# Attention into two gated layers: softmax sums applied where layer 1 loads x, and six w_out chunks homed with the first layer's w_in

## The chip, the cores and the metric

The kernel runs on one core of one Trainium2 chip. The metric is the device time of one execution in microseconds (us). The engines are TensorE (PE), VectorE (DVE), ScalarE (ACT), GpSimd (POOL) and SyncE (SP); SP issues every DMA of this kernel.

## What is computed

The cut reference: windowed causal attention in fp32 (batch 4, 8 heads, 576 tokens, 64 columns a head, window 128), whose output x of 2304 x 512 goes through a layer with a rational gate and then one with a squared ReLU.

```python
scores = np.where(mask, scale * q @ k.T + bias, -1e9)
attn = np.exp(scores - scores.max(-1))
attn = attn / (attn.sum(-1) + 1e-09)
x = (attn @ v)                       # to (2304, 512)
h = x @ w_in                         # 512 x 2048
g = (a0 + a1*h + a2*h**2 + a3*h**3) / (1 + |b0|*|h| + |b1|*h**2 + 1e-6)
x = g @ w_out                        # 2048 x 512
out = (np.maximum(x @ w2_in, 0)**2) @ w2_out
```

## The kernel before

**Attention** runs in 16 pairs p (batch, two heads) of five query blocks, called units u, 80 in all. For a pair, q, k and v are loaded (`qr`, `kr`, `vr`; three DMAs each, L285 and L292), q and k are transposed on PE (`trq`, `trk`, `trr`) and copied to `qkT`. For a unit, PE makes the scores `s` (L340); DVE adds bias and mask from the table `bias8` and takes the minimum (L351); ACT makes the exponentials `e` with their row sum (L360); DVE turns the sum into a reciprocal (`stats` L368, `rcp` L370); POOL multiplies `e` by it (`norm`, L375, two a unit); PE transposes `e` to `pt` (L391); ACT or DVE copies that to `ptsb`; PE multiplies by v into `o` and, for the last 64 tokens of a pair, `or` (L416 to L429). The copied result `xT` of a pair goes to DRAM as `xs` (L443).

**The layers** run in blocks of up to 512 tokens, 16 steps f a block, the first layer's block 1 of 256. A step makes h (`gemm_in`, L614, twelve matmuls of 512 columns, since operands are split into a high and a low part), the gate on ACT, POOL and DVE, the high part `gh` on ACT and the low part `gl` on DVE (L214), and adds to y (`gemm_out`, L698, twelve matmuls). PSUM has four banks for s and h together, so h of step f+4 waits for `gl` of step f, the last reader of its bank. x of a block is read back from DRAM (`load_x`, tile `xr`, L594) once all pairs that make it are written.

**Weights** come raw as 64-bit numbers, 64 chunks of 512 KB (`win1r`, `wout1r`, ..., L185), and are rebuilt as fp32: `w_exp` on any engine (L191, L194), three bit operations on DVE (L199, L201, L203), the high part (L207, L211), the low part (L214). The 16 chunks of w_in of the first layer are converted during attention. Their home is the pool `wip`. w_out's home `wop` is opened by `attn_end`, in the space that the attention pools free, so its conversion writes nothing before attention's last copies.

**Order.** The class Plan simulates all pieces with a cost for each and puts down, for every engine, one static order; each engine then runs its instructions in that order and waits where an operand is missing. SP is planned at 0.45 us a DMA. A table BIAS decides between pieces that could start at the same time.

Of the kernel before, what the change touches and what calls it, by code (L numbers as in the profile page):

```python
# [8 lines left out]
F32 = mybir.dt.float32  # L9
# [80 lines left out]
BIAS = {'W0': 1143.4, 'W1': -1312.0, 'W2': -103.0, 'W3': 231.6, 'attn_end': -330.6, 'bias': -108.4, 'exp': -122.1, 'g1': 74.7, 'g2': 539.3, 'gh': -139.2, 'gl': -251.1, 'ldk': 347.8, 'ldk0': -524.7, 'ldq': -531.4, 'ldq0': -320.3, 'ldv': 478.2, 'norm': -28.5, 'ptc': 550.8, 'ptp': -190.6, 'pv': 8.0, 'r_abs': -768.2, 'r_g1': 208.6, 'r_g2': -228.1, 'r_g3': -464.7, 'r_p1': -223.8, 'r_p2': -200.3, 'r_r1': -323.9, 'r_r2': -709.6, 'r_t1': 437.4, 'r_t2': 344.1, 'r_u': -364.3, 'rcp': -339.7, 's': 671.8, 's_g': -202.9, 's_relu': 313.4, 'scl': 1.6, 'scp': -406.8, 'stats': -279.6, 'trk': -947.3, 'trk0': 180.7, 'trk0c': -287.8, 'trkc': -54.6, 'trq': -411.2, 'trq0': 156.9, 'trq0c': 381.4, 'trqc': 386.6, 'trr': -605.2, 'trrc': -29.2, 'ttr': -13.0, 'w0': -272.4, 'w1': 518.7, 'w2': -17.8, 'w3': -48.3, 'w4': -107.7, 'w5': -1964.8, 'warm': 652.0, 'wl': -312.2, 'x': 515.5, 'xh': 551.8, 'xl': 139.5, 'xld': 247.8, 'xo': -326.7, 'xr': -322.8, 'yc': 281.2, 'yo': 224.4}  # L90
# [4 lines left out]
VB, TRO = 3, 0  # L95
# [3 lines left out]
def tile_window_attention_moe_moe(  # L99
# [43 lines left out]
    ]  # L143

# [98 lines left out]
    bias8 = acst.tile([P, H, 2 * P], F32, name="bias8")  # L243
# [26 lines left out]
    st = {}  # L270


    def parts(p, nme):
        return [(0, 2), (2, NQ - 1)] if p == 0 and nme != "v" else [(0, NQ - 1)]

    def load_tok(p, nme, src, t0, t1):
# [12 lines left out]
        if t1 == NQ - 1:

            rows = slice(P - LAST, P) if nme == "v" else slice(0, LAST)
            nc.sync.dma_start(  # L292
                t[rows, t1, :, :],
                src[b, h0 : h0 + 2, MAIN:, :].rearrange("h p d -> p h d"),
            )


    def tr_main_pe(p, nme, t0, t1):
        ps = bank("tr", f"tr{nme}{p}_{t0}")
        src = st[p][nme]  # L300
        for t in range(t0, t1):
            nc.tensor.transpose(  # L302
                ps[:, t * P : (t + 1) * P], src[:, t].rearrange("p h d -> p (h d)"), ident
            )
        if "qkT" not in st[p]:
            st[p]["qkT"] = ap2.tile([P, 2, S], F32, tag="qkT", name=f"qkT{p}")
        cs = slice(t0 * P, t1 * P)
        st[p]["trps"] = (ps[:, cs], st[p]["qkT"][:, "qk".index(nme), cs])

    def tr_rem_pe(p):  # L310
        ps = bank("tr", f"trr{p}")
        for n, nme in enumerate("qk"):
# [29 lines left out]
    def ttr(u, j):  # L342
# [4 lines left out]
        if j == 0:  # L347
            d["st"] = ae.tile([P, 8], F32, tag="st", name=f"st{u}")
            d["e"] = ae.tile([P, 2, 2 * P], F32, tag="e", name=f"e{u}")
        b0 = P if i == 0 else 0  # L350
        nc.vector.tensor_tensor_reduce(  # L351
            d["e"][:rows, j, :w], d["s"][j], bias8[:rows, h, b0 : b0 + w],
            -0.125, 1e30, ALU.add, ALU.min, d["st"][:rows, j : j + 1],
        )

    def exp(u, j):
        d = us[u]
        rows, w, s = d["rows"], d["w"], d["st"]
        e = d["e"][:rows, j, :w]
        nc.scalar.activation(  # L360
            e, e, AF.Exp, scale=-1.0, bias=s[:rows, j : j + 1],
            accum_out=s[:rows, 2 + j : 3 + j],
        )

    def stats(u, k):
        rows, s = us[u]["rows"], us[u]["st"]
        if k == 0:
            nc.vector.tensor_scalar(s[:rows, 4:6], s[:rows, 2:4], 1e-9, None, ALU.add)  # L368
        else:
            nc.vector.reciprocal(s[:rows, 4:6], s[:rows, 4:6])  # L370
# [33 lines left out]
    def pv_pe(u):  # L404
# [4 lines left out]
        if i == NQ - 1:  # L409
            st[p]["or"] = bank("tr", f"or{p}")  # L410
# [39 lines left out]
    for p in range(NP):  # L450
# [5 lines left out]
        for n, (nme, src) in enumerate((("q", q), ("k", k), ("v", v))):  # L456
            if n == 2:
                busy = [("pv", u0 - VB * NQ + NQ - 1)]
            else:
                busy = [("trr", p - 2)]  # L460
            for t0, t1 in parts(p, nme):
                part = "" if t1 == NQ - 1 else "0"
# [25 lines left out]
        plan.add(  # L488
            ("trr", p), lambda p=p: tr_rem_pe(p), PE=0.2,
            after=[("trkc", p), ("xr", p - 2)], prio=u0 - 3,  # L490
        )
        plan.add(("trrc", p), lambda eng, p=p: tr_copy(p, eng), ACT=0.16, DVE=0.2, after=[("trr", p)], prio=u0 - 3)
# [364 lines left out]
```

## Time and profile before

| | |
|---|---|
| time, median of 3 runs | 952.62 us (952.4 to 954.46) |
| profiled execution, time | 952.25 us |
| profiled execution, span | 950.5 us |
| PE busy | 935.9 us |
| DVE busy | 627.5 us |
| ACT busy | 495.0 us |
| POOL busy | 395.0 us |

Attention fills the first 150 us or so, the two layers the rest. The span is what the hardware profiler saw of the program; the profiled execution's own time is 1.75 us longer. The profile's views used below: the page (busy time, chain of work that ended last, groups of instructions), a table by stretch, the waits of an engine, the timeline of single instructions, and the DMA issues.

### The profile page before, as it was taken

Reading aid. Unit: us, or ns where it says so; the run is one execution under the profiler, and the core shown is the slowest. Engines: PE = TensorE matmul, PEld = TensorE weight load, DVE = VectorE, ACT = ScalarE, POOL = GpSimd, SP = SyncE. Lnnn points to the kernel's source line nnn. Section 1 sums busy time; section 2 is a strip of 40 time slices with the busy share of each in tenths; the row PEclk is TensorE's granted clock in tenths of the full one; section 3 lists DMA queues with packets and bytes.
Section 4 is the critical chain, followed back from the end, with each engine's and each line's share of the span. In section 5 each row is a group of like instructions: output and inputs, shape, how many; then the busy total and the mean of one; then the engine's idle time right before and its main releaser. Section 6 shows DMA issues by size and latency. Waiting matters only on the chain.

```text
span 950.5 us, 14368 instructions
## 1 busy us (share of the span) xinstructions
PE 935.9 (98%) x4940; PEld 760.1 (80%) x4940; DVE 627.5 (66%) x1436; ACT 495.0 (52%) x1089; POOL 395.0 (42%) x481
## 2 busy tenths in 40 slices
PE   8999999899999999999999999999999999999998
PEld 6666667688998888888888888888888888888887
DVE  5999999999987877777999977762222223222332
ACT  5888896667776655655676543432222222222222
POOL 5787887677555436334767753230010001000100
PEclk9999999999999999999999999999999999999999
DMA  6989763222401100200142236412000200010010
GB/s 150 239 203 231 205 169 101 90 83 92 154 22 37 32 1 1 89 1 1 45 136 87 66 117 197 130 45 90 0 1 1 89 1 0 35 33 1 1 45 23
DMA packets 96521, 72.24 MB, mean 76 GB/s; under 512 B 61888, under 2 KB 84416, under 8 KB 96448
## 3 DMA queue, kind: packets, MB, share of 16 engines
q1 hardware_dynamic: 96448, 71.33, 26.3%
q8 instruction: 39, 0.64, 0.3%
q14 instruction: 34, 0.28, 0.1%
HBM read 57.15 MB, written 14.16 MB: 75 GB/s over the span
## 4 chain that ended last, share of the span: by engine, by line
PE 90%; DVE 6%; POOL 1%; ACT 1%; issue 1%; DMA 1%; POOLq 0%; ACTq 0%; DVEq 0%
PE y L698 40%; PE h L614 40%; PE s L340 3%; PE pt L391 3%; PE o L416 2%; DVE e L351 1%; PE warm L549 1%; POOL e L375 1%; DVE h L667 1%; PE trk L302 1%; PE trq L302 1%; ACT e L360 1%; DVE wb L203 1%; DVE wb L201 0%; DMA win1r<-in_moe_w_in_dram 0%
## 5 line engine op out<-in xcount | busy, mean ns | idle before, releaser
L214 DVE TENSOR_TENSOR gl<-h,gh 128x512 fp32r<-128x512 f32 (+1 forms) x160 | 101.1, 633 | 115.3 <-ACT gh L207 115.2
L207 ACT ACTIVATE gh<-h 128x512 fp32r<-128x512 f32 (+1 forms) x160 | 88.5, 554 | 162.4 <-PE y L698 152.7
L675 DVE SCALAR_TENSOR_TENSOR h<-h,ah 128x512 f32<-128x512 f32 (+1 forms) x80 | 51.6, 645 | 112.5 <-ACT ah L671 112.5
L614 PE MATMUL h<-xh,win1hi 128*128 128x512 f32 (+1 forms) x320 | 119.0, 372 | 4.6 <-DVE gl L214 4.6
L211 POOL TENSOR_SCALAR xh<-xr 128x512 fp32r<-128x512 f32 (+1 forms) x20 | 12.5, 629 | 255.5 <-PE h L614 253.9
L614 PE MATMUL h<-xl,win1hi 128*128 128x512 f32 (+1 forms) x320 | 118.4, 370 | 0.1
L614 PE MATMUL h<-xh,win1lo 128*128 128x512 f32 (+1 forms) x320 | 118.2, 369 | 0.0
L614 PE MATMUL h<-xh,win2hi 128*128 128x512 f32 (+1 forms) x320 | 117.9, 368 | 0.0
L614 PE MATMUL h<-xh,win2lo 128*128 128x512 f32 (+1 forms) x320 | 117.7, 368 | 0.0
L698 PE MATMUL y<-gl,wout1hi 128*128 128x512 f32 (+1 forms) x320 | 117.7, 368 | 0.0
L698 PE MATMUL y<-gh,wout1hi 128*128 128x512 f32 (+1 forms) x320 | 117.7, 368 | 0.0
L614 PE MATMUL h<-xl,win2hi 128*128 128x512 f32 (+1 forms) x320 | 117.7, 368 | 0.0
L698 PE MATMUL y<-gh,wout1lo 128*128 128x512 f32 (+1 forms) x320 | 117.7, 368 | 0.0
L698 PE MATMUL y<-wout2hi,gh 128*128 128x512 f32 x288 | 112.1, 389 | 0.0
L698 PE MATMUL y<-wout2hi,gl 128*128 128x512 f32 x288 | 112.1, 389 | 0.0
L639 POOL TENSOR_SCALAR t<-ah,ab_sb 128x512 f32<-128x512 f32 (+1 forms) x80 | 64.2, 803 | 115.2 <-ACT ah L627 98.8
L698 PE MATMUL y<-wout2lo,gh 128*128 128x512 f32 x288 | 112.0, 389 | 0.0
L671 ACT ACTIVATE ah<-h 128x512 f32<-128x512 f32 (+1 forms) x80 | 44.4, 554 | 122.9 <-PE h L614 122.7
L641 POOL TENSOR_TENSOR t<-t,ah 128x512 f32<-128x512 f32 (+1 forms) x80 | 99.8, 1247 | 6.2
L375 POOL TENSOR_SCALAR e<-e,st 128x256 f32<-128x256 f32 (+2 forms) x160 | 85.4, 549 | 29.2 <-ACT e L360 12.0
L627 ACT ACTIVATE ah<-h 128x512 f32<-128x512 f32 (+1 forms) x80 | 44.2, 553 | 64.5 <-PE h L614 64.0
L647 DVE TENSOR_TENSOR u<-u,h 128x512 f32<-128x512 f32 (+1 forms) x80 | 50.3, 629 | 39.1 <-ACT u L631 39.0
(114 smaller groups left out, 1991.8 us busy)
## 6 DMA issues: line engine op xcount, KB each, us to landing
win1r<-in_moe_w_in_dram SPq DMA_DIRECT2D x16, 512.0 KB, 4.3
wout1r<-in_moe_w_out_dram SPq DMA_DIRECT2D x16, 512.0 KB, 3.4
win2r<-in_moe_w_in_dram SPq DMA_DIRECT2D x16, 512.0 KB, 3.7
wout2r<-in_moe_w_out_dram SPq DMA_DIRECT2D x16, 512.0 KB, 3.4
xs<-xT SPq DMA_DIRECT2D x16, 288.0 KB, 3.0
out_dram<-yt SPq DMA_DIRECT2D x18, 256.0 KB, 2.1
vr<-in_v_dram SPq DMA_DIRECT2D x32, 128.0 KB, 4.1
ys<-yt SPq DMA_DIRECT2D x16, 256.0 KB, 4.2
```

What stands on the lines that cost most here:

```text
L207: nc.scalar.activation(dst, src, AF.Copy)
L214: (nc.vector if eng == "DVE" else nc.gpsimd).tensor_tensor(dst, a, b, ALU.subtract)
L340: nc.tensor.matmul(dst[j], qT[js, qs], kT[js, k0:k1], start=True, stop=True)
L375: nc.gpsimd.tensor_scalar(e, e, d["st"][: d["rows"], 4 + j : 5 + j], 1.0, ALU.mult, ALU.mult)
L614: nc.tensor.matmul(h[:, :n], a[:, c * P : (c + 1) * P], bb[:, :n], start=(m == 0), stop=(m == 3 * NCC - 1),)
L627: nc.scalar.activation(gt("ah", 2, ji, f), tl["h", ji, f], AF.Abs)
L639: nc.gpsimd.tensor_scalar(gt("t", 2, ji, f), ah, ab_sb[:, 1:2], ab_sb[:, 0:1], ALU.mult, ALU.add)
L641: nc.gpsimd.tensor_tensor(tl["t", ji, f], tl["t", ji, f], ah, ALU.mult)
L647: nc.vector.tensor_tensor(u, u, h, ALU.mult)
L671: nc.scalar.activation(gt("ah", 2, ji, f), tl["h", ji, f], AF.Relu)
L675: nc.vector.scalar_tensor_tensor(h, h, 0.0, tl["ah", ji, f], ALU.max, ALU.mult)
L698: nc.tensor.matmul(dst, a, bb, start=(f == 0 and m == 0), stop=(f == NF - 1 and m == 2))
```

## The change

1. The reciprocal is no longer applied to `e`. `norm` and the two small DVE operations of each unit go. `exp` puts its row sums in a table `sums[p % 3]` (128 x 10); once a pair two DVE operations make the reciprocals `rc`, PE transposes them (into the free part of `or`), ACT or DVE copies them to `rt`, and a DMA writes them to DRAM (`rs`, 16 DMAs). `load_x` of the first layer also loads them, spread over the 64 rows of a head, as tile `R` (two DMAs for each DMA of `xr`), and `norm_x` multiplies `xr` by `R` on DVE or POOL.
2. `wop0` is a home for the first six chunks of w_out that exists from the start; `wop` keeps the other ten. To make room, `e` lives in the tiles of `gh` and `gl`, and the bias table in those of `ah` and `t`.
3. v's loads are planned on their own, the dependences are adapted, BIAS has other values.

```diff
-BIAS = {'W0': 1143.4, 'W1': -1312.0, 'W2': -103.0, ...
+BIAS = {'W0': 149.1, 'W1': 54.9, 'W2': -317.0, ...
...
+    NE = 6
+    wop0 = ctx.enter_context(tc.tile_pool(name="wop0", bufs=NE))
...
-        pool = pools[nme[:-1]]
+        pool = wop0 if nme[:-1] == "wout" and f < NE else pools[nme[:-1]]
...
-    bias8 = acst.tile([P, H, 2 * P], F32, name="bias8")
+    bias8 = [
+        gp.tile([P, 2, 2 * P], F32, tag="at"[k % 2] + "h" * (k % 2 == 0), name=f"bias{k}", bufs=2)
...
-            d["e"] = ae.tile([P, 2, 2 * P], F32, tag="e", name=f"e{u}")
+            d["e"] = gp.tile([P, 2, 2 * P], F32, tag=("gh", "gl")[u % 2], name=f"e{u}", bufs=3)
...
-            accum_out=s[:rows, 2 + j : 3 + j],
-        )
...
-        nc.gpsimd.tensor_scalar(
-            e, e, d["st"][: d["rows"], 4 + j : 5 + j], 1.0, ALU.mult, ALU.mult
-        )
+            e, e, AF.Exp, scale=-1.0, bias=s[:rows, j : j + 1], accum_out=sums[p % 3][:rows, c : c + 1],
+        )
+
+    def rcp(p):
+        t = st[p]["rc"] = ap2.tile([P, 2 * NQ], F32, tag="rc", name=f"rc{p}")
+        nc.vector.tensor_scalar(t, sums[p % 3], 1e-9, None, ALU.add)
+        nc.vector.reciprocal(t, t)
+
+    def r_tr(p):
+        st[p]["or"] = bank("tr", f"or{p}")
+        nc.tensor.transpose(st[p]["or"][: 2 * NQ, P : 2 * P], st[p]["rc"], ident)
+
+    def r_copy(eng, p):
+        t = st[p]["rt"] = ap2.tile([2 * NQ, P], F32, tag="rt", name=f"rt{p}")
+        copy(eng, t, st[p]["or"][: 2 * NQ, P : 2 * P])
+
+    def r_out(p):
+        nc.sync.dma_start(rs[p], st[p]["rt"])
...
-        pools["wout"] = ctx.enter_context(tc.tile_pool(name="wop", bufs=NF))
+        pools["wout"] = ctx.enter_context(tc.tile_pool(name="wop", bufs=NF - NE))
...
+        if jobs[ji][0] == "a":
+            t = tl["R", ji, c] = xp.tile([P, T], F32, tag="R", name=f"R{ji}_{c}", bufs=2)
+            for d, m, _, _, r, q0 in runs(ji, c):
+                for j in range(2):
+                    nc.sync.dma_start(
+                        t[j * D : (j + 1) * D, d : d + m],
+                        bass.AP(tensor=r.tensor, offset=r.offset + j * NQ * P + q0, ap=[[0, D], [1, m]]),
+                    )
+
+    def norm_x(eng, ji, c):
+        n = jobs[ji][2]
+        xr = tl["xr", ji, c][:, :n]
+        (nc.vector if eng == "DVE" else nc.gpsimd).tensor_tensor(xr, xr, tl["R", ji, c][:, :n], ALU.mult)
...
-            0: [], 1: [("attn_end",)], 2: [("g1", NB1 - 1, f)], 3: [("g2", NB1 - 1, f)],
+            0: [], 1: [] if f < NE else [("attn_end",)], 2: [("g1", NB1 - 1, f)], 3: [("g2", NB1 - 1, f)],
```

**POOL, from attention's end into the first gate.** The names: `e` with a number is a unit's exponentials, `t0_0` the denominator of block 0's step 0, `wb` a weight chunk in conversion. Before:

```order
L375 TENSOR_SCALAR e74_2463<-e74_2463,st74_2462 64x192 x2
L375 TENSOR_SCALAR e75_2495<-e75_2495,st75_2494 128x128 x2
L375 TENSOR_SCALAR e76_2507<-e76_2507,st76_2506 128x256 x2
L375 TENSOR_SCALAR e77_2550<-e77_2550,st77_2549 128x256 x2
L375 TENSOR_SCALAR e78_2554<-e78_2554,st78_2553 128x256 x2
L375 TENSOR_SCALAR e79_2578<-e79_2578,st79_2577 64x192 x2
L639 TENSOR_SCALAR t0_0_2651<-ah0_0_2634,ab_sb_96 128x512
L641 TENSOR_TENSOR t0_0_2651<-t0_0_2651,ah0_0_2634 128x512
```

Six units' multiplications stood ahead of `t0_0`. With the change POOL reads there:

```order
L199 TENSOR_SCALAR wb17_2392<-wout1r_1_2312 128x512
L216 TENSOR_SCALAR wout1hi_1_2441<-wb17_2392 128x512
L219 TENSOR_TENSOR wout1lo_1_2442<-wb17_2392,wout1hi_1_2441 128x512
L199 TENSOR_SCALAR wb18_2475<-wout1r_2_2382 128x512
L219 TENSOR_TENSOR wout1lo_2_2531<-wb18_2475,wout1hi_2_2530 128x512
L199 TENSOR_SCALAR wb19_2536<-wout1r_3_2450 128x512
L680 TENSOR_SCALAR t0_0_2550<-ah0_0_2544,ab_sb_115 128x512
L682 TENSOR_TENSOR t0_0_2550<-t0_0_2550,ah0_0_2544 128x512
```

The multiplications of `e` are gone; weight pieces, w_out's among them, stand in their place, and one of them is the row just ahead of `t0_0`.

**DVE, from `gl` of block 0's step 1 to `gl` of step 2.** `u`, `t` and `h` with block and step are the gate's tiles; `wb` and `wout1r` belong to a chunk of w_out. Before, the last twelve of the fourteen rows that end with `gl0_2`:

```order
L203 SCALAR_TENSOR_TENSOR wb18_2823<-wout1r_2_2723,wb18_2823 128x512
L667 SCALAR_TENSOR_TENSOR t0_2_2768<-t0_2_2768,h0_2_2706 128x512
L647 TENSOR_TENSOR u0_4_2850<-u0_4_2850,h0_4_2774 128x512
L667 SCALAR_TENSOR_TENSOR h0_2_2706<-t0_2_2768,h0_2_2706 128x512
L649 SCALAR_TENSOR_TENSOR u0_4_2850<-u0_4_2850,ca_sb_93,h0_4_2774 128x512
L667 SCALAR_TENSOR_TENSOR h0_2_2706<-u0_2_2766,ca_sb_93,h0_2_2706 128x512
L667 SCALAR_TENSOR_TENSOR t0_3_2820<-t0_3_2820,h0_3_2744 128x512
L667 SCALAR_TENSOR_TENSOR h0_3_2744<-t0_3_2820,h0_3_2744 128x512
L201 SCALAR_TENSOR_TENSOR wb19_2880<-wb19_2880,wout1r_3_2795 128x512
L667 SCALAR_TENSOR_TENSOR h0_3_2744<-u0_3_2790,ca_sb_93,h0_3_2744 128x512
L203 SCALAR_TENSOR_TENSOR wb19_2880<-wout1r_3_2795,wb19_2880 128x512
L214 TENSOR_TENSOR gl0_2_2900<-h0_2_2706,gh0_2_2888 128x512
```

Two steps' gates and the chunks 2 and 3 were mixed there. With the change DVE goes from `gl0_1` to `gl0_2` in eight rows:

```order
L219 TENSOR_TENSOR gl0_1_2725<-h0_1_2571,gh0_1_2703 128x512
L708 SCALAR_TENSOR_TENSOR h0_2_2612<-t0_2_2658,h0_2_2612 128x512
L690 SCALAR_TENSOR_TENSOR u0_3_2695<-u0_3_2695,ca_sb_112,h0_3_2639 128x512
L688 TENSOR_TENSOR u0_4_2727<-u0_4_2727,h0_4_2676 128x512
L708 SCALAR_TENSOR_TENSOR h0_2_2612<-u0_2_2656,ca_sb_112,h0_2_2612 128x512
L690 SCALAR_TENSOR_TENSOR u0_4_2727<-u0_4_2727,ca_sb_112,h0_4_2676 128x512
L206 SCALAR_TENSOR_TENSOR wb21_2701<-wb21_2701,wout1r_5_2569 128x512
L219 TENSOR_TENSOR gl0_2_2756<-h0_2_2612,gh0_2_2752 128x512
```

From `gl0_0` to `gl0_2` there were 26 rows, eight of them conversions of w_out's chunks 1 to 3, and now there are 18, four of them conversions (chunks 4 and 5).

**SP, around the loads of pair 8.** `qr8`, `kr8`, `vr8` are its q, k and v, `xr1_0` is block 1's first quarter of x, `xs` a pair's result; in the second piece `rs` and `R` are the new transfers. Before:

```order
L285 DMA qr8_1128<-in_q_dram 128x4x64 x2
L292 DMA qr8_1128<-in_q_dram 64x2x64
L285 DMA kr8_1160<-in_k_dram 128x4x64 x2
L292 DMA kr8_1160<-in_k_dram 64x2x64
L185 DMA win1r_7_1194<-in_moe_w_in_dram 128x4x256
L594 DMA xr1_0_1206<-xs0_0_71 128x64
L594 DMA xr1_0_1206<-xs1_0_75 128x192
L285 DMA vr8_1234<-in_v_dram 128x4x64 x2
L292 DMA vr8_1234<-in_v_dram 64x2x64
L443 DMA xs1_1_76<-xT5_1232 128x576
```

With the change SP reads, from the same load on:

```order
L291 DMA qr8_1108<-in_q_dram 128x4x64 x2
L295 DMA qr8_1108<-in_q_dram 64x2x64
L291 DMA kr8_1134<-in_k_dram 128x4x64 x2
L295 DMA kr8_1134<-in_k_dram 64x2x64
L190 DMA win1r_7_1159<-in_moe_w_in_dram 128x4x256
L401 DMA rs5_95<-rt5_1171 10x128
L621 DMA xr1_0_1193<-xs0_0_74 128x64
L621 DMA xr1_0_1193<-xs1_0_78 128x192
L627 DMA R1_0_1196<-rs0_90 64x64 x2
L627 DMA R1_0_1196<-rs4_94 64x192 x2
L304 DMA vr8_1242<-in_v_dram 128x4x64 x2
L308 DMA vr8_1242<-in_v_dram 64x2x64
```

x2 stands for two DMAs. Between q of pair 8 and q of pair 9 there were 13 DMAs, and now there are 17; from q of pair 4 to q of pair 12 there were 99, and now there are 128; ahead of q of pair 4 there were 46, and now there are 47.

## Rows read from the trace of the kernel before

**Rows 1.** The page: TensorE's busy time, and the chain that ended last.

```profile
PE 935.9 (98%) x4940; PEld 760.1 (80%) x4940; DVE 627.5 (66%) x1436; ACT 495.0 (52%) x1089; POOL 395.0 (42%) x481
...
PE 90%; DVE 6%; POOL 1%; ACT 1%; issue 1%; DMA 1%; POOLq 0%; ACTq 0%; DVEq 0%
```

**Rows 2.** Table by stretch: length; busy PE, PEld, DVE, ACT, POOL; PE clock; DMA share; GB/s.

```profile
20.00:150.00 130.00, 127.06 (x1065) 82.67 (x1064) 123.51 (x574) 112.21 (x392) 105.53 (x177) 1.00 0.81 202
160.00:200.00 40.00, 35.96 (x152) 29.00 (x151) 38.81 (x66) 28.65 (x48) 29.14 (x28) 0.96 0.27 88
200.00:300.00 100.00, 99.38 (x608) 89.09 (x607) 89.04 (x184) 69.58 (x148) 61.62 (x71) 1.00 0.24 75
```

**Rows 3.** What TensorE waited for: total us, times, longest.

```profile
PE h L614 <- DVE gl L214: 4.6, 3, 2.8
PE pt L391 <- POOL e L375: 1.7, 5, 0.6
```

**Rows 4.** Timeline of TensorE, attention's end and after: start, length, instruction, [idle before].

```profile
167.16 0.39 PE L698 MATMUL y<-gh,wout1lo 128*128 128x512 f32 x1
168.76 0.50 PE L614 MATMUL h<-xh,win1hi 128*128 128x512 f32 x1 [1.21 <-DVE gl L214]
...
174.11 0.39 PE L698 MATMUL y<-gh,wout1lo 128*128 128x512 f32 x1
177.33 0.79 PE L614 MATMUL h<-xh,win1hi 128*128 128x512 f32 x1 [2.83 <-DVE gl L214]
...
244.29 0.39 PE L614 MATMUL h<-xh,win1hi 128*128 128x256 f32 x1 [0.53 <-DVE gl L214]
```

**Rows 5.** The chain that ended last, two pieces: start, length, work.

```profile
177.33 7.09 PE h L614 x24
184.43 2.72 PE y L698 x12
```

**Rows 6.** Timeline of DVE: `gl` of steps 0, 1, 2 (with 3).

```profile
160.66 0.68 DVE L214 TENSOR_TENSOR gl<-h,gh 128x512 fp32r<-128x512 f32 x1
...
168.02 0.69 DVE L214 TENSOR_TENSOR gl<-h,gh 128x512 fp32r<-128x512 f32 x1
...
176.59 1.28 DVE L214 TENSOR_TENSOR gl<-h,gh 128x512 fp32r<-128x512 f32 x2
```

**Rows 7.** Timeline of POOL and ACT at the first gate.

```profile
146.90 4.83 POOL L375 TENSOR_SCALAR e<-e,st 128x256 f32<-128x256 f32 x6 [1.37 <-DVE xT L266]
...
148.97 0.60 ACT L627 ACTIVATE ah<-h 128x512 f32<-128x512 f32 x1
...
151.72 1.23 POOL L639 TENSOR_SCALAR t<-ah,ab_sb 128x512 f32<-128x512 f32 x1
```

**Rows 8.** The page, groups: busy us, mean ns, idle before and its releaser.

```profile
L375 POOL TENSOR_SCALAR e<-e,st 128x256 f32<-128x256 f32 (+2 forms) x160 | 85.4, 549 | 29.2 <-ACT e L360 12.0
```

**Rows 9.** Timeline of TensorE: groups of four and two transposes; q of pair 12.

```profile
107.54 0.66 PE L302 MATMUL trq<-ident,qr 128*128 128x128 f32 x4
...
148.77 0.62 PE L391 MATMUL pt<-ident,e 128*128 128x128 f32 x4
149.94 0.44 PE L391 MATMUL pt<-ident,e 128*128 128x128 f32 x2 [0.55 <-POOL e L375]
```

**Rows 10.** Timeline of SP's issues: q of pairs 4 and 12; xs, xs, xr between.

```profile
29.14 1.01 SPq L285 DMA_DIRECT2D qr<-in_q_dram  x2
...
63.18 0.53 SPq L443 DMA_DIRECT2D xs<-xT  x1
...
80.95 0.54 SPq L443 DMA_DIRECT2D xs<-xT  x1
...
93.35 1.07 SPq L594 DMA_DIRECT2D xr<-xs  x2
...
98.63 0.98 SPq L285 DMA_DIRECT2D qr<-in_q_dram  x2
```

**Rows 11.** DMA issues from 60 to 112 us: count, KB each, median us to landing.

```profile
qr<-in_q_dram SPq DMA_DIRECT2D x12, 128.0 KB, 4.2
```

More of the change, by code (lines that the diff above doesn't have):

```diff
@@ L143, in tile_window_attention_moe_moe @@
     ]
+    NPP = B * NPAIR
+    rs = [dram.tile([2 * NQ, P], F32, tag=f"rs{p}", name=f"rs{p}") for p in range(NPP)]
     nc.scalar.preload_act_table_set("natural_log_exp_and_others")
@@ L269, in tile_window_attention_moe_moe, with parts, load_qk @@
     NP = len(pairs)
[L270 to L276, printed above, removed]
+    st = {p: {} for p in range(NP)}
+    def parts(p):
+        return [("0", 0, 2), ("", 2, NQ - 1)] if p == 0 else [("", 0, NQ - 1)]
+    def load_qk(p, nme, src, t0, t1):
         b, hp = pairs[p]
@@ L453, in tile_window_attention_moe_moe @@
         at = {"prio": u0}
[L456 to L462, printed above, removed]
+        for n, (nme, src) in enumerate((("q", q), ("k", k))):
+            for part, t0, t1 in parts(p):
                 w = (t1 - t0) / (NQ - 1)
@@ L487, in tile_window_attention_moe_moe @@
                 last = (tr + "c", p)
[L488 to L492, printed above, removed]
+        plan.add(("trr", p), lambda p=p: tr_rem(p), PE=0.2, after=[last, ("xr", p - 2)], prio=u0 - 3)
+        plan.add(("trrc", p), lambda eng, p=p: tr_copy(eng, p), ACT=0.16, DVE=0.2, after=[("trr", p)], prio=u0 - 3)
         for g in range((NQ + 1) // 2):
@@ L758, in tile_window_attention_moe_moe @@
         for c in range(NCC):
-            srcs = [d for r in runs(ji, c) for d in r[3:]]
-            old = [("yo", ji - 2, c), ("yo", ji - 2, NCC - 1), ("xld", ji, c - 1)]
+            nr = len(runs(ji, c))
+            srcs = [d for r in runs(ji, c) for d in r[3]]
+            old = [("xn", ji - (c < 2), (c - 2) % NCC), ("yo", ji - 2, c), ("yo", ji - 2, NCC - 1), ("xld", ji, c - 1)]
             plan.add(
-                ("xld", ji, c), lambda ji=ji, c=c: load_x(ji, c), SP=0.45 * len(srcs), move=0.75 * sc,
+                ("xld", ji, c), lambda ji=ji, c=c: load_x(ji, c), SP=0.45 * nr * (3 if kind == "a" else 1), move=0.75 * sc * (2 if kind == "a" else 1),
                 after=srcs + old + [("yc", ji - 2, c), ("xl", ji - 1, c)], prio=p0 - 20 + c,
             )
+            if kind == "a":
+                plan.add(
+                    ("xn", ji, c), lambda eng, ji=ji, c=c: norm_x(eng, ji, c), DVE=per(0.33, 0.6), Pool=per(0.69, 1.23),
+                    after=[("xld", ji, c)], prio=p0 - 6 + c, port=True,
+                )
             plan.add(
@@ L780, in tile_window_attention_moe_moe @@
             if s < 4:
-                after += [("s", NP - 1, 2), ("ttr", NU - 1 - (s < 2), 1), ("exp", NU - 1, 1)]
+                after += [("s", NP - 1, 2), ("exp", NU - 1, 1)] + [("ttr", NU - 1 - u, 1) for u in range(NQ)]
             pc = prev(4)
@@ L814, in tile_window_attention_moe_moe @@
                 after += [("yc", ji - 1, i) for i in range(NCC)]
+                if ji == 0:
+                    after += [("xr", p) for p in range(NP)] + [("ptc", NU - 1 - u) for u in range(NQ)]
             plan.add(
```

142 lines of the change are left out of this document (77 added, 65 removed).

## The prediction

> **What bounds the kernel now.** I read the page first: TensorE is busy for 935.9 of 950.5 us and holds 90% of the chain that ended last, DVE 6% [rows 1]. A gain can therefore come only from stretches in which PE stands idle or runs slowly, and the table by stretch says where these are [rows 2]. From 20 to 150 us, in attention, PE is busy for 127.06 of 130 us, so 2.94 us are open. From 160 to 200 us it has 35.96 of 40 and a granted clock of 0.96. From 200 to 300 us it has 99.38 of 100, and what follows runs matmul behind matmul; there is nothing to win there. Third, the waits of PE: 4.6 us in three pieces for `gl` on DVE, and 1.7 us in five pieces for the normalized `e` on POOL [rows 3]. So two places count: the start of the first layer, which waits for DVE, and attention, which waits a little for POOL.
>
> **The start of the first layer, removed.** PE's timeline shows each of the three pieces [rows 4]. Matmuls there follow one another at 0.23 us (twelve take 2.72 [rows 5]). The last y matmul before the first gap starts at 167.16 and the next h at 168.76: 1.60 - 0.23 = 1.37 us lost. The second pair is 174.11 and 177.33: 3.22 - 0.23 = 2.99 us. Behind that gap 24 matmuls take 7.09 us [rows 5] where two times 2.72 = 5.44 would do, 1.65 us more: the first starts with 0.79 us instead of 0.39, and the stretch has the lower mean clock [rows 2, 4]. So the lower level of 1.2 GHz follows directly on the idle piece and goes with it. A last wait of 0.53 us stands at 244.29 [rows 4]. Together 1.37 + 2.99 + 1.65 + 0.53 = 6.5 us.
>
> Do these go? DVE is busy for 38.81 of the 40 us from 160 on [rows 2], so PE waits for a backlog and not for a latency. `gl0_0` starts at 160.66, `gl0_1` at 168.02, the pair `gl0_2`, `gl0_3` at 176.59 [rows 6]. From the first to the third there are 26 rows in DVE's order, so 15.93 / 26 = 0.61 us each. In the new order there are 18, which is 11.0 us: four conversions of w_out are gone from between (2.4 us), and the steps no longer come in twos, so four rows of later steps are out of the way too. That alone brings `gl0_2` 4.9 us forward. Second, `gl0_0` itself comes earlier: POOL's last six norms run without a break from 146.90 to 151.73 and `t0_0` starts at 151.72, though `ah0_0` was written at 148.97 + 0.60 = 149.57 [rows 7]. With the norms gone and at most one conversion piece in front, about 2.1 us of this chain fall away. `gl0_2` comes some 7 us earlier where 1.37 + 2.99 = 4.36 are needed, and `gl0_3` follows ten rows, 6.1 us, behind it against a pace of two times 2.72 = 5.44. The margin is 2 to 3 us, the cover that would have to fail. What is late next is the conversion of chunks 4 to 15, which DVE still does beside the gate. I take back 6.0 us of the 6.5 and leave 0.5 for a wait of that kind.
>
> **Attention, removed.** 160 norms take 85.4 us of POOL's time [rows 8], nearly all beside other work; what lay on the path is the 1.7 us of waits [rows 3] and the part of the 2.94 us that a looser chain closes. Ends: 1.7 and 2.94. I take 2.3 us. The 160 small reciprocal steps on DVE become 32, and their time goes to twelve bit operations of four w_out chunks; DVE is no faster through attention and need not be. Copies of `pt` and q, k move from DVE to ACT, which is busy for 112.21 of 130 us [rows 2] and has room for about 10 us more. These edits cost nothing as long as ACT stays under the stretch's length.
>
> **Attention, added on PE.** Sixteen transposes of `rc`. Four transposes run in 0.62 us and two in 0.44 [rows 9], so one more takes 0.09 us: 16 x 0.09 = 1.4 us. The ends are nothing (they fill gaps) and 16 x 0.155 = 2.5 us (0.62 / 4). The last product of a pair now also waits for the reciprocal, but its own transposes wait for the same exponentials, so I price this wait at zero; queued behind it on PE would be the next pair's scores.
>
> **Attention, added on SP.** Here the change costs. Every DMA goes through SP, and ahead of `q` of pair 12 there are 29 more than before (128 for 99 from q of pair 4 on), one `rs` a pair and two or four `R` for each quarter of x. Before, SP issues q of pair 4 at 29.14 and q of pair 12 at 98.63 [rows 10], and between 63.18 and the end of the last `xr` issue at 93.35 + 1.07 = 94.42 it puts out 48 DMAs: 31.24 / 48 = 0.651 us each. In the calmer part from 80.95 it is 23 in 13.47 us: 0.586 us each. PE uses q of pair 12 at 107.54 [rows 9], 8.9 us after its issue, of which 4.2 us are the transfer [rows 11]: the slack is 4.7 us. With the change q of pair 4 has one DMA more ahead of it, 29.7 us. Then q of pair 12 lands at 29.7 + 128 r + 4.2, which is 108.9 us at r = 0.586 and 117.2 us at r = 0.651. Lowest, with only the 29 new ones at the 0.54 us of a plain `xr` issue (1.07 for two [rows 10]): 58.0 + 15.7 + 33.9 = 107.6 us. PE, unhindered, would be there at 107.54 - 1.5 + 1.1 = 107.1 us (two thirds of the norm term, twelve transposes). The delay has the ends 0.5 and 10.1 us. I take r = 0.595, near the calm end since most new DMAs are small, which lands q at 110.1: a delay of 3.0 us, kept to the end of attention because nothing behind pair 12 gives it back.
>
> The Trainium skill, page "DMA: Bandwidth & Descriptors", section "Issuing engines are not separate DMA queues", holds that the sequencer time of starting a DMA is usually small relative to the DMA. By that the SP term would be nil and the time that of the first rival; this trace speaks against it, since the 0.586 us between issues come back 128 times while the 4.2 us of a transfer overlap [rows 10, 11].
>
> Edits with one answer: the four multiplications by `R` of block 0 and four of block 1 fall on POOL, which the norms left with 85 us of room; later ones stand beside matmuls. `R` adds to a DMA share of 0.81 [rows 2], which leaves room. Nothing.
>
> **The sum.** 952.25 (the profiled execution; it lies 0.37 us under the median 952.62) - 6.0 - 2.3 + 1.4 + 3.0 = 948.35, say 948.4 us.
>
> **Rivals.** First, SP is hidden: it ran ahead, and the waits inside its stretch absorb the new issues. Then the 3.0 us fall away: 945.4 us, and 942.7 with the transposes free and all 2.94 and 6.5 us regained. For it: the unhindered estimate misses by only 0.5 us.
>
> Second, slower: SP becomes what attention runs at. At r = 0.651 q of pair 12 is at 117.2 us, 9.7 us behind PE's 107.54 of before. The norm's gain is swallowed by that, the transposes too, and the start still gives 6.0: 952.25 + 9.7 - 6.0 = 956.0 us. It decides against the change from 107.54 + 6.0 on, which is r = (113.5 - 33.9) / 128 = 0.622 us per DMA. For it: the mean of 48 issues lies above that [rows 10]; against it: part of that mean is waiting for others.
>
> Third, the change does not do what it says: the first layer still starts behind a backlog, because DVE, at 123.51 of 130 us in attention [rows 2], or ACT, with the copies it took over, arrives late, or because the four conversions left between `gl0_0` and `gl0_2` do what eight did. With half of the 6.0 regained the time is 951.4 us, with none 954.4.
>
> **How the numbers follow.** Forecast 42%, from 946.5 to 950.8. SP hidden 22%, from 942.7 to 946.5. Backlog 19%, from 949.5 to 954.5. SP bound 17%, from 952 to 957. A measurement of this kernel can tell 0.2% from no change, 1.9 us: faster ends at 950.7 and slower begins at 954.5 against the median. Faster: 0.38 + 0.22 + 0.05 = 0.65; same: 0.04 + 0.12 + 0.05 = 0.21; slower: 0.02 + 0.12 = 0.14. The range runs from 942.7 to 955.0 and leaves out the far ends of the SP cases.
>
> **What would show it.** Right: PE has no wait for `gl` over 1 us at the start of the first layer and its clock stays at 1.00 there; DVE has 18 instructions between those two `gl`; waits for POOL in attention are gone; `trq` of a pair between 9 and 13 waits for a DMA, 2 to 5 us in all; SP issues without a pause there. Wrong: `trq` never waits (first rival), or attention ends over 6 us later (second), or h still waits for `gl` (third).

## The result, and the profile after

The changed kernel takes 959.41 us against 952.68 for the kernel before: 1.0064 times as long, 95% interval 1.0047 to 1.0082. Faster was forecast; it is slower. The profiled execution took 959.43 us, its span is 957.7.

The start of the first layer did what was predicted, and more. Attention lost twice that. One row from each kernel separates the two: the first matmul of h of block 0. Before (timeline of PE):

```profile
145.94 0.48 PE L614 MATMUL h<-xh,win1hi 128*128 128x512 f32 x1
```

and after:

```profile
161.68 0.48 PE L655 MATMUL h<-xh,win1hi 128*128 128x512 f32 x1
```

Attention hands over 15.7 us later; over 6 was the prediction's sign of its second rival. From there to the end of the span it was 950.5 - 145.94 = 804.6 us, and now it is 957.7 - 161.68 = 796.0: 8.5 us less. (Four transposes of `pt` and a few small pieces have changed sides of this row, under 1 us.) These two lengths, like every stretch below, come from one profiled execution of each kernel. The table by stretch of the changed kernel, columns as in [rows 2]:

```profile
20.00:150.00 130.00, 117.00 (x960) 76.80 (x958) 101.81 (x411) 107.26 (x370) 44.33 (x46) 0.96 0.84 210
80.00:100.00 20.00, 17.61 (x127) 11.80 (x128) 14.34 (x56) 14.41 (x51) 3.35 (x4) 0.83 0.75 191
100.00:120.00 20.00, 17.62 (x144) 11.38 (x142) 11.91 (x56) 15.51 (x52) 5.16 (x6) 0.91 0.68 170
160.00:200.00 40.00, 40.00 (x208) 32.15 (x207) 37.69 (x68) 27.86 (x52) 29.34 (x29) 1.00 0.24 83
200.00:300.00 100.00, 99.69 (x609) 89.79 (x608) 92.86 (x186) 68.73 (x146) 63.37 (x72) 1.00 0.28 85
```

From 160 us on PE is full and its clock stays at 1.00. In attention, where [rows 2] had 127.06 us of PE work and 123.51 of DVE, there are 117.00 and 101.81, and the granted clock has fallen to 0.83 between 80 and 100 us. No engine is fuller than before (the DMA share is 0.84 for 0.81), so attention is held by something that is not an engine's work. The waits of PE (total, times, longest) are short and scattered:

```profile
PE o L438 <- ACT ptsb L272: 3.0, 3, 2.4
PE or L394 <- DVE qkT L274: 2.7, 3, 1.5
PE or L394 <- ACT qkT L272: 2.5, 2, 1.8
...
PE tr L320 <- DMA qr<-in_q_dram: 1.2, 2, 0.6
...
PE h L655 <- DVE gl L219: 0.3, 1, 0.3
```

and the chain that ended last, 90% PE in [rows 1], now runs through DMA and SP's queue:

```profile
PE 79%; DVE 9%; DMA 5%; SPq 2%; ACT 2%; POOL 1%; issue 1%; ACTq 0%; DVEq 0%; POOLq 0%
```

`gl` has gone from 4.6 us [rows 3] to 0.3, and no row is left of PE's 1.7 us for POOL. PE hardly waits for `q`: 1.2 us, where the prediction's sign was 2 to 5. One engine back, DVE's waits from 20 to 160 us name the cause; this line has no counterpart before:

```profile
DVE wb L199 <- DMA win1r<-in_moe_w_in_dram: 15.0, 8, 3.8
```

How such a wait comes about is seen in the chain that ended last, between 105 and 114 us:

```profile
104.97 0.63 SPq L295
...
105.65 5.23 DMA win1r<-in_moe_w_in_dram
...
110.97 0.43 DVE wb L199
111.40 0.34 DVE win1r L204
111.74 0.33 DVE e L365
...
112.17 0.60 ACT e L381 x2
112.77 0.49 ACT ptsb L272
...
113.31 0.92 PE o L438 x4
```

SP finishes issuing k of a pair, only then issues a w_in chunk, and the chunk takes 5.23 us to land. DVE stands in its fixed order in front of the chunk's first operation, with attention's `e` right behind it. `e` needs nothing from the chunk; it waits because of its place. ACT waits for `e`, PE for ACT. SP's own rows for q of pairs 4 and 12, as in [rows 10]:

```profile
30.29 1.12 SPq L291 DMA_DIRECT2D qr<-in_q_dram  x2
...
112.75 1.08 SPq L291 DMA_DIRECT2D qr<-in_q_dram  x2
```

128 DMAs in 82.46 us are 0.644 us each, where the 99 of before took 69.5 us, 0.702 each. The difference is in the pauses. SP's own rows between these two add up to 74.4 us of issuing here and to 58.3 us before, 0.58 and 0.59 us a DMA; pauses over 0.15 us there are three here, 1.8 us in all, and six before, 6.1 us in all. So SP was already issuing most of the time, and with the 29 new DMAs it hardly ever stops.

### The profile page after: what moved, and what is told of

Read it like the earlier page. It is cut to its first block, busy times and chain, and to the rows that moved or that the text cites. A ratio compares the mean times of both kernels' runs of the same rounds, so it can differ in the third digit from the quotient of the medians.

```text
span 957.7 us, 14275 instructions
## 1 busy us (share of the span) xinstructions
PE 936.8 (98%) x4956; PEld 762.3 (80%) x4956; DVE 621.2 (65%) x1304; ACT 500.6 (52%) x1104; POOL 330.9 (35%) x349
## 4 chain that ended last, share of the span: by engine, by line
PE 79%; DVE 9%; DMA 5%; SPq 2%; ACT 2%; POOL 1%; issue 1%; ACTq 0%; DVEq 0%; POOLq 0%
PE h L655 37%; PE y L739 37%; DMA win1r<-in_moe_w_in_dram 3%; DVE h L708 2%; PE o L438 1%; DVE wb L206 1%; PE pt L415 1%; SPq L291 1%; PE s L354 1%; DVE gl L219 1%; DVE t L708 1%; DVE wb L208 1%; DVE u L688 1%; PE tr L320 1%; DVE e L365 1%
## 5 line engine op out<-in xcount | busy, mean ns | idle before, releaser
L712 ACT ACTIVATE ah<-h 128x512 f32<-128x512 f32 (+1 forms) x80 | 44.4, 555 | 117.7 <-PE h L655 117.2
L682 POOL TENSOR_TENSOR t<-t,ah 128x512 f32<-128x512 f32 (+1 forms) x80 | 97.8, 1223 | 5.3
L381 ACT ACTIVATE e<-e,st 128x256 f32<-128x256 f32 (+2 forms) x160 | 74.5, 470 | 11.6 <-DVE st L365 10.8
L655 PEld LDWEIGHTS h<-xh,win1hi 128*128 128x128 f32 x320 | 60.3, 189 | 10.6 <-DVE gl L219 0.5
L655 PEld LDWEIGHTS h<-xh,win2hi 128*128 128x128 f32 x320 | 60.3, 188 | 10.6
```

The costliest lines, as they stand in the source:

```text
L381: nc.scalar.activation(e, e, AF.Exp, scale=-1.0, bias=s[:rows, j : j + 1], accum_out=sums[p % 3][:rows, c : c + 1],)
L655: nc.tensor.matmul(h[:, :n], a[:, c * P : (c + 1) * P], bb[:, :n], start=(m == 0), stop=(m == 3 * NCC - 1),)
L682: nc.gpsimd.tensor_tensor(tl["t", ji, f], tl["t", ji, f], ah, ALU.mult)
L712: nc.scalar.activation(gt("ah", 2, ji, f), tl["h", ji, f], AF.Relu)
```

## The experiments

Theory A: SP's time for issuing the added DMAs holds attention up. Rivals: B, the new static order (conversions that begin on DVE ahead of attention's work); C, the sums' path through PE, DVE and ACT; A', the bytes and short rows of R rather than the count. For each run I read the median time, the issue of q of pair 12 on SP, and the start of layer 1. The kernel before took 952.0 to 952.6 us beside the runs.

**The R loads left out.**

```
-            for d, m, _, _, r, q0 in runs(ji, c):
-                for j in range(2):
-                    nc.sync.dma_start(
...
-        (nc.vector if eng == "DVE" else nc.gpsimd).tensor_tensor(xr, xr, tl["R", ji, c][:, :n], ALU.mult)
+        (nc.vector if eng == "DVE" else nc.gpsimd).tensor_tensor(xr, xr, xr, ALU.mult)
```

> The changed kernel without the loads of R (left out: the division by the softmax sums; xr is multiplied by itself, so every instruction but the R loads stays in its place). From q of pair 4 to q of pair 12 this leaves 104 DMAs instead of 128. Theory A (SP issues too slowly, 0.644 us a DMA, and what comes late is a w_in chunk that DVE stands waiting for): q of pair 12 is issued near 30.3 + 104 x 0.644 = 97 us instead of 112.75, DVE's waits for win1r fall from 16.0 us to under 3, the time is 945 to 949 us. Theory B (the static order is at fault: nine conversions of w_in begin on DVE ahead of attention's own work, whatever SP does): the waits stay above 10 us and the time above 955 us. Theory C (the sums' path through PE, DVE and ACT itself costs the time): no change, 957 to 960 us.

946.4 us, ratio to before 0.9937 (0.9915 to 0.9959): 13.0 us less than the changed kernel. SP's rows:

```profile
30.37 0.99 SPq L291 DMA_DIRECT2D qr<-in_q_dram  x2
...
102.97 0.94 SPq L291 DMA_DIRECT2D qr<-in_q_dram  x2
```

The time is where A put it, but not all of the expected readings came. DVE's waits for chunks fell to 10.5 us, not under 3, and SP took 72.6 us for its 104 DMAs, not 67. The profiled execution took 949.45 us, 3 us more than the median, so its rows overstate what is left. B and C fall as main causes; whether it is the count or the bytes this run can't say.

**The count kept, the bytes taken away.**

```
-                        t[j * D : (j + 1) * D, d : d + m],
-                        bass.AP(tensor=r.tensor, offset=r.offset + j * NQ * P + q0, ap=[[0, D], [1, m]]),
+                        t[j * D : (j + 1) * D, d : d + 2],
+                        bass.AP(tensor=r.tensor, offset=r.offset + j * NQ * P + q0, ap=[[0, D], [1, 2]]),
```

> The changed kernel with each R load cut to two columns (left out: the division by the sums; xr is multiplied by itself). The number of DMAs and the order of every engine stay, the bytes of R all but go. Theory A, the count of issues: q of pair 12 stays at 111 to 114 us and the time within 956 to 960 us. Theory A', the bytes of R in the DMA engines: near the run without R, 946 to 949 us.

957.75 us, as A had it. The count of issues costs; the bytes are worth about 1.7 us. SP's rows show the same pace as in the changed kernel, 81.3 us for 128 DMAs:

```profile
29.82 1.25 SPq L291 DMA_DIRECT2D qr<-in_q_dram  x2
...
111.16 1.08 SPq L291 DMA_DIRECT2D qr<-in_q_dram  x2
```

This is the cleanest pair of the study: two kernels with the same order of every instruction but the DMAs themselves. With the R issues, however small, 957.75; without them 946.4.

**The new DMAs alone, in the kernel before.**

```
...
             nc.sync.dma_start(xr[:, d : d + m], src)
+        if jobs[ji][0] == "a":
+            t = xp.tile([P, T], F32, tag="R", name=f"R{ji}_{c}", bufs=2)
+            for d, m, _, _ in runs(ji, c):
+                for j in range(2):
+                    nc.sync.dma_start(
+                        t[j * D : (j + 1) * D, d : d + m],
+                        bass.AP(tensor=q.tensor, offset=q.offset + j * NQ * P, ap=[[0, D], [1, m]]),
+                    )
...
+        nc.sync.dma_start(rs[p], st[p]["x"][: 2 * NQ, :P])
         nc.sync.dma_start(xs[b][hp], st.pop(p)["x"])
```

> The kernel before with the new transfers only: one rs write per pair and two R-shaped loads for each load of xr in layer 1, into a tile that nobody reads. Nothing else is changed; 131 DMAs instead of 99 from q of pair 4 to q of pair 12. Theory A: q of pair 12 is issued near 29.8 + 131 x 0.644 = 114 us, PE uses it 8 to 11 us later than before, the time is 958 to 963 us. Theory B: the old order lets DVE begin only two w_in chunks, so the time stays within 952 to 955 us. Theory C: 952 to 953 us.

970.63 us, ratio 1.0185 (1.0160 to 1.0209): 18 us lost by transfers that nobody reads, more than A's 958 to 963. 131 DMAs took 86.4 us, 0.660 each, and here PE does wait for q:

```profile
29.52 1.24 SPq L286 DMA_DIRECT2D qr<-in_q_dram  x2
...
115.93 1.00 SPq L286 DMA_DIRECT2D qr<-in_q_dram  x2
```
```profile
PE pt L392 <- POOL e L376: 6.0, 8, 2.7
PE h L624 <- DVE gl L215: 4.8, 4, 2.8
PE trq L303 <- DMA qr<-in_q_dram: 3.2, 1, 3.2
```

The old order has no immunity, so B falls for good. In this order the wait shows on PE and POOL and less on DVE (2.3 us for chunks).

**The first conversion step kept off DVE.**

```
-            ("w0", n), lambda eng, n=n: w_exp(eng, n), ACT=0.56, Pool=0.6, DVE=0.34,
+            ("w0", n), lambda eng, n=n: w_exp(eng, n), ACT=0.56, Pool=0.6, **({"DVE": 0.34} if n >= NF else {}),
```

> The changed kernel with the first step of a w_in chunk's conversion kept off DVE (ACT or POOL do it: 5 and 11 chunks); the 128 DMAs stay. Theory A: SP still reaches q of pair 12 at 110 us or later, the wait moves to another place (q on PE, bit operations on DVE), 953 to 960 us. Theory B: DVE no longer stands still, 945 to 950 us.

961.65 us, 1.65 above A's range and far from B's. SP's pace is unchanged (q of pair 12 at 111.25 us), and DVE waits one instruction further on:

```profile
DVE win1r L204 <- DMA win1r<-in_moe_w_in_dram: 12.7, 9, 2.1
```

**The R loads on other engines.** The same DMAs, in the same places of the program, issued by GpSimd; in the other run `nc.scalar` stands there:

```
-                    nc.sync.dma_start(
+                    nc.gpsimd.dma_start(
```

> The changed kernel, complete, with the R loads issued by GpSimd instead of SP; the order of every other instruction stays, as do the count and bytes of the transfers. 104 DMAs are left on SP from q of pair 4 to q of pair 12. If the cost is SP's time for issuing: q of pair 12 at 101 to 105 us, 946 to 950 us, like the run without R. If it is the number of transfers in the shared DMA engines: 956 us or more. Rival to the gain: POOL stands still for each issue and its descriptors, and the w_in pieces behind it come late, 951 to 956 us.

> The same with the R loads issued by ScalarE. ACT was busy for 107 of the 130 us from 20 to 150 and waits in its order for rs to land, ahead of exponentials. SP relieved: q of pair 12 at 101 to 105 us; but each of the eight groups of R loads holds up ACT by 0 to 2 us, so 948 to 956 us, behind the GpSimd run by 2 us or more.

GpSimd: 953.9 us, 5.5 less than the changed kernel though every transfer still runs, so at least that much of the loss was the issuer's. q of pair 12 came at 103.63 us, within the 101 to 105 expected if SP's issuing is the cost, but the time lies in the range of the rival, in which POOL stands still. The start of layer 1 moved from 161.68 to 153.31 us. Behind it there is a new loss from 250 to 300 us, where this run has 47.24 us of PE work and the changed kernel 49.69. POOL's timeline shows it:

```profile
258.63 0.56 POOL L680 TENSOR_SCALAR t<-ah,ab_sb 128x256 f32<-128x256 f32 x1 [2.18 <-DVE h L708]
259.13 2.13 POOL L627 DMA_DIRECT2D R<-rs  x4
261.25 0.77 POOL L682 TENSOR_TENSOR t<-t,ah 128x256 f32<-128x256 f32 x1
```

Four issues, 0.53 us each, stand between the two halves of a gate operation. ScalarE: 962.52 us, worse than SP and above the expected 948 to 956; q of pair 12 came at 111.44 us and not at 101 to 105. ACT pays about 0.6 us an issue, ahead of the exponentials:

```profile
94.91 0.45 ACTq L627 DMA_DIRECT2D R<-rs  x1
95.40 1.90 ACTq L627 DMA_DIRECT2D R<-rs  x3
```

**GpSimd for attention's R loads only, then for `rs` too** (the last two lines, in the second run alone).

```
-                    nc.sync.dma_start(
+                    (nc.gpsimd if ji < 2 else nc.sync).dma_start(
...
-        nc.sync.dma_start(rs[p], st[p]["rt"])
+        nc.gpsimd.dma_start(rs[p], st[p]["rt"])
```

> The changed kernel, complete, with the R loads of blocks 0 and 1 issued by GpSimd (they fall in attention) and those of the later blocks by SP again. If the 5 us that the run with all R loads on GpSimd lost between 250 and 300 us came from POOL issuing them between its gate operations, they go: 947 to 950 us, faster than both kernels. If they came from something else: 952 to 955 us as in that run.

> The same with the sixteen rs writes on GpSimd too, which leaves 96 DMAs on SP from q of pair 4 to q of pair 12, fewer than the 99 of the kernel before. Issue count as the cost: 1 to 3 us below the run with R alone on GpSimd. If the remaining loss is POOL's: the same or slower, since POOL waits in its order for each rt.

950.55 us, ratio 0.9987 (0.9976 to 0.9998), just above the expected 947 to 950, and 949.74 us, ratio 0.9981 (0.9971 to 0.9990). With every transfer of the changed kernel in place, 8.9 us of its time are gone, most of the 13.0 that the R loads cost. What the other 4 us are (950.55 - 946.4: the transfers, POOL's time for the issues, waits for R) was not taken apart. The loss between 250 and 300 us is gone (first line: all R on GpSimd; second: the last version):

```profile
250.00:300.00 50.00, 47.24 (x346) 45.16 (x345) 38.37 (x92) 30.69 (x77) 33.74 (x49) 0.97 0.25 75
```
```profile
250.00:300.00 50.00, 49.79 (x372) 47.67 (x371) 42.98 (x99) 34.14 (x82) 28.86 (x35) 1.00 0.26 75
```

The last version computes everything and is faster than both kernels: 9.7 us under the changed one, 2.4 us under the one before. The step from the first to the second is 0.8 us, less than the expected 1 to 3 and within the uncertainty of the two: with 104 DMAs left, taking eight more off SP gains next to nothing.

**Merging, and moving in time.** The R loads of four quarters as one, in all blocks and then in blocks 0 and 1 alone:

```
-                        bass.AP(tensor=r.tensor, offset=r.offset + j * NQ * P + q0, ap=[[0, D], [1, m]]),
+        if jobs[ji][0] == "a" and c == NCC - 1:
...
+                        t[j * D : (j + 1) * D, :, lo - t0 : hi - t0],
+                        bass.AP(tensor=r.tensor, offset=r.offset + j * NQ * P + lo - b * S, ap=[[0, D], [2 * NQ * P, NCC], [1, hi - lo]]),
```

> The changed kernel with the R loads of the four quarters of x merged into one pair of DMAs for each run of tokens (the same bytes in the same row lengths, a quarter of the issues): 108 DMAs instead of 128 from q of pair 4 to q of pair 12. Theory A, with the count of issues as the cost: 945 to 950 us, DVE's waits for win1r under 4 us. Theory A', with the bytes or the short rows of R as the cost (they slow the w_in loads from 4.3 to 5.1 us): 955 us or more and w_in loads above 5 us still. Theory B: above 955 us.

> The changed kernel, complete, with the R loads of blocks 0 and 1 alone merged (one pair of DMAs for each run of tokens instead of four); later blocks load R quarter by quarter as the changed kernel does. 108 DMAs from q of pair 4 to q of pair 12. Issues as the cost: attention ends 8 to 11 us earlier than in the changed kernel, 948 to 952 us. If the merged loads come too late for block 0: waits of POOL or DVE for R ahead of the first layer, 953 to 958 us.

969.28 and 968.71 us, far outside A's ranges and above the second run's rival too. The first time alone would fit A' and B, but the w_in loads took 4.3 us to land and not over 5, as A' would have it, and B has fallen. SP is relieved (q of pair 12 at 104.63 and 105.02 us), but R now comes with the last quarter only, and DVE waits for it in its order; the plan, made anew, also puts w_out's conversions later, which PE meets in the first layer. From the second of the two, DVE first:

```profile
DVE xr L652 <- DMA R<-rsb: 7.1, 2, 4.1
```
```profile
PE s L355 <- DVE st L366: 4.0, 2, 3.6
PE h L672 <- DVE gl L220: 3.6, 5, 1.6
PE y L756 <- POOL wout1lo L220: 2.4, 3, 1.2
...
PE y L756 <- POOL wout1hi L217: 1.5, 1, 1.5
```

Fewer issues do not help when the one that is left comes too late. Block 1's loads held back until the last v:

```
-                after=srcs + old + [("yc", ji - 2, c), ("xl", ji - 1, c)], prio=p0 - 20 + c,
+                after=srcs + old + [("yc", ji - 2, c), ("xl", ji - 1, c)] + ([("ldv", NP - 1)] if ji == 1 else []), prio=p0 - 20 + c,
```

> The changed kernel, complete, with the loads of x and R for block 1 held back until the last load of v has been issued: 108 DMAs from q of pair 4 to q of pair 12. Theory A: q of pair 12 is issued at 99 to 102 us, DVE's waits for win1r halve at least, 946 to 951 us. Rival: the same SP work then stands between the w_out loads at the start of layer 1 and is paid there, 955 us or more.

956.95 us: the rival's case. Attention is mended (layer 1 starts at 149.30 us, 12.4 earlier than in the changed kernel), but the stretch from there to the end is 954.7 - 149.30 = 805.4 us, the whole gain of the early home lost. The held-back loads now stand between the w_out loads: the fourth of these is issued 9.0 us after the start of layer 1, and in the changed kernel 4.4 us ahead of it. PE waits there for `gl`:

```profile
PE h L655 <- DVE gl L219: 5.8, 6, 2.0
```

**One part alone.** First w_out's high and low parts after attention, with the sums on the loads (the edit below); then the early home with `stats`, `rcp` and `norm` of the kernel before in place of `rcp`, `r_tr`, `r_copy`, `r_out`, R and `norm_x`.

```
-            0: [], 1: [] if f < NE else [("attn_end",)], 2: [("g1", NB1 - 1, f)], 3: [("g2", NB1 - 1, f)],
+            0: [], 1: [("attn_end",)], 2: [("g1", NB1 - 1, f)], 3: [("g2", NB1 - 1, f)],
```

> The changed kernel with the high and low parts of all w_out chunks made only after attention again; the sums stay on the x loads and the 128 DMAs stay. Theory A: attention keeps its delay of about 13 us and the waits for gl at the start of layer 1 come back, 962 to 967 us. Rival: since attention runs late, DVE has time to spare and the early home gives nothing, 958 to 960 us.

> The changed kernel with the sums applied as before (reciprocal per query block, multiplication of e on POOL, no rs, no R), so that only the early home of six w_out chunks and of the bias table is left; 101 DMAs from q of pair 4 to q of pair 12. Theory A: no wait for DMA in attention, the start of layer 1 keeps most of its gain, 946 to 949 us. Rival: the bit operations of w_out that now stand on DVE in attention, which was 95% busy there, give the gain back, 951 to 956 us.

980.04 us, above both ranges: attention as late as in the changed kernel (162.55 us), and from there to the end 978.0 - 162.55 = 815.5 us instead of 796.0. In this order, planned anew with the BIAS of the changed kernel, the early home is worth 19 us; against the order of the kernel before it was 8.5. The early home alone, 960.28 us and above both ranges too, is inconclusive: its plan had to be made anew, and it came out with loads of v ahead of q, for whose buffers SP stands still:

```profile
SPq L304 <- PE pt L405: 15.4, 8, 3.6
```

With the norms back on POOL, PE still waits 4.0 us for `gl` in it. So neither part alone gives the gain at the start of layer 1, and this run doesn't price the home by itself.

**The whole path of the sums left out.** The R loads and `norm_x` as in the run without R, and besides:

```
-        nc.tensor.transpose(st[p]["or"][: 2 * NQ, P : 2 * P], st[p]["rc"], ident)
...
-        copy(eng, t, st[p]["or"][: 2 * NQ, P : 2 * P])
...
-        nc.sync.dma_start(rs[p], st[p]["rt"])
```

> The changed kernel without the whole path of the sums behind the reciprocals: no transposes of rc, no copies rt, no rs, no R (left out: the division by the sums; xr is multiplied by itself). All other instructions stay in their order. Without R alone the first matmul of layer 1 started at 151.62 us, against 145.94 before and 161.68 in the changed kernel. If the rest of that delay is PE's wait for the one bank that the rc transposes share with those of q and k (5.2 us in the changed kernel), plus the transposes' own 1.4 us and the sixteen rs: start at 145.5 to 148 us, time 940 to 943.5 us. If it is the new order of loads and conversions: start at 150 to 152 us, 945 to 947 us.

945.17 us, 1.2 us under the run without R alone. Layer 1 starts at

```profile
146.81 0.47 PE L645 MATMUL h<-xh,win1hi 128*128 128x512 f32 x1
```

0.9 us after the kernel before. The start lies in the first band and the median in the second. Since the profiled execution without R took 3 us more than its median, I go by medians: transposes, copies and `rs` cost 1.2 us together, and the new order as such about 1.

## Why the prediction was wrong

The account, from medians and the two stretches: 952.4 before; -8.5 from the start of layer 1 on; +1.3, the remainder, for attention in its new order (945.2 - 943.9); +1.2 for transposes, copies and `rs` (946.4 - 945.2); +13.0 for the R loads on SP (959.4 - 946.4, about 1.7 of it their bytes). Sum 959.4, which it must be, since one term is what the others leave.

- **The start of layer 1, -6.0.** Right: `gl` waits went from 4.6 to 0.3 us, and the low clock behind the gap is gone. By the tables, PE's idle time and its low clock from 160 to 300 us were (40 - 35.96) + 0.04 x 40 + (100 - 99.38) = 6.3 us [rows 2] and are 0.3. The other 2.5 us of the 8.5 are pieces that changed sides (under 1 us), 0.7 us of waits for POOL just behind the start of layer 1, and a rest that no row here shows.
- **The norms, -2.3.** PE's waits for POOL went, but no gain in attention is seen: without the sums' path layer 1 starts 0.9 us later than before, not 2 us earlier. Whether the new order used the gain up was not tested.
- **The transposes of `rc`, +1.4.** Near in size for the whole path, 1.2. The wait that I priced at zero, the last product's for the reciprocal, is in no row of PE's. But the path has waits that the prediction does not name: the transposes share the one bank `tr` with those of q and k, and PE waited 5.2 us there in the changed kernel (`or` for `qkT`, 2.7 and 2.5), 1.7 without R.
- **SP, +3.0: the step that failed.** The R loads alone cost 13.0 us, over four times the term. The mechanism stood there; the size was wrong in three ways. First the rate: of 0.586 and 0.651 us I chose 0.595, since most new DMAs are small. At that rate 128 DMAs pass in 76 us, only 6.7 more than the 99 took [rows 10], so the term let the old DMAs go over 10 us faster than they had. The changed kernel shows 0.644, and the run with R cut to two columns 0.635: the R loads, though small, cost SP 0.62 us each, and the mean stays high though SP pauses for only 1.8 us. By the prediction's own line, 0.644 puts q of pair 12 at 116.3 us, 8.8 behind 107.54 and beyond the 6.0 from which the change loses. The second rival had the mechanism, and at 956.0 it was still 3.4 us short. Second the place: I followed q alone, whose slack is 4.7 us, and PE hardly waited for it. What came late was the w_in chunk behind k, which stands on DVE ahead of attention's work. `tr` of pair 12's q ran at 120.0 us, 12.5 us later than 107.54 [rows 9]. Third the clock: rows of the changed kernel show a lower granted clock in the stretches that wait, which I had not counted in attention.
- **"Nothing" for the other edits.** A conversion on DVE was priced by its busy time, and not by what is queued behind it when its load is late. DVE waited 15.0 us for chunks, and the prediction's list of added waits had only PE's. Without the sums' path, in otherwise the same order, these waits are 4.1 us and the time is 945.17, so the conversions' places cost much only when SP is late.
- The rule that the time to start a DMA is usually small beside the DMA (the Trainium skill, "DMA: Bandwidth & Descriptors", section "Issuing engines are not separate DMA queues") fits one R load here, 0.62 us of SP against 2.7 to 4.4 us from issue to landing, but not the sum that the prediction's sentence drew from it. The 24 R loads in attention cost 11 us even when cut to two columns (957.75 - 946.4). The same section says that issuing from another engine saves the issuer's time only; with the R loads of blocks 0 and 1 on GpSimd that came to 8.9 us.

## What to carry to other kernels

Count the DMAs that one engine must issue in a stretch, multiply by the longest mean interval that the trace shows under load, and compare it with the stretch's length: here 0.651 us [rows 10] gives 83 us for the 128 DMAs, where SP took 82.5, and the 99 of before had taken 69.5. A conversion or a prefetch that stands in an engine's fixed order is a promise that its load has landed; price what is queued behind it, not its own length. If issues must be added, give them to an engine with time to spare in that stretch, and take them back where that engine is on the path.

## What the runs showed that I had not expected

**Fewer bytes do not make an R load cheaper to issue.** Two R loads of 512 columns (128 KB each) and four of 64 and 192 (16 and 48 KB), on SP in the changed kernel:

```profile
36.24 1.12 SPq L627 DMA_DIRECT2D R<-rs  x2
...
75.91 2.39 SPq L627 DMA_DIRECT2D R<-rs  x4
```

That is 0.56 and 0.60 us each. All 24 R loads of attention took SP 0.62 us each on average, and 0.62 again in the run with two columns, where a load moves 0.5 KB. GpSimd took 0.53 and ScalarE 0.63 in the rows above. What stands behind an issue in the engine's order starts after it: ACT's next exponential at 97.36 us, when the three issues end at 97.30. Not every issue is this long: `rs` (5 KB) took 0.43 us on average and the loads of x 0.41. What makes the difference these runs don't show; the bytes don't.

**Up to about 108 DMAs SP is not the limit.** From q of pair 4 to q of pair 12 the runs with 96, 104 and 108 DMAs on SP (the last version, without R, block 1 late) took 73.3, 72.6 and 72.6 us: the time does not follow the count. The two merged runs (108 DMAs) took 74.6 and 75.3, and the one with ScalarE (104) 81.1; other waits held these up. With 128, 128 and 131, in the changed kernel, with two columns and in the kernel before with the DMAs added, it was 82.5, 81.3 and 86.4 us, 0.635 to 0.660 each.

**The clock fell behind two waits in attention.** In the changed kernel the granted clock is 0.83 from 80 to 100 us, a mean of the levels 1.2 and 2.4 GHz: by stretches of 2 us it is 1.00 up to 92 us, 0.50 (1.2 GHz) from 94 to 98, and 1.00 again from 100 on. PE had stood idle for 1.55 us up to 91.81. It is 0.50 again from 114 to 116 us, behind the 2.38 us for which PE stood idle up to 113.31. The same group of eight matmuls of scores, at the lower level and at the upper:

```profile
95.88 2.08 PE L354 MATMUL s<-qkT 64*128 64x256 f32 x8
```
```profile
105.92 1.13 PE L354 MATMUL s<-qkT 64*128 64x256 f32 x8
```

By the table's clock column, 0.17 and 0.09 of two stretches of 20 us, the clock is worth up to (0.17 + 0.09) x 20 = 5.2 us of the delay (an estimate: what PE would have done in that time it may have had to wait for). The run without R has 1.00 in both.
